# Moving the roots' write, three key transfers and four weight pieces to other places in the queues

## The chip, the cores and the metric

The kernel runs on one core of one Trainium2 chip. The metric is the device time of one execution in microseconds. The engines are TensorE (PE), VectorE (DVE), ScalarE (ACT), GpSimd (POOL) and SyncE (SP); transfers are issued by SP or by POOL, each of which has its own queue, and are carried out by 16 DMA engines.

## The reference

```python
def _attn_ref(q, k, v, g_norm):          # 8 images, 8 heads, 576 tokens, 64 wide
    kv = np.einsum('bhsd,bhse->bhde', k, v)
    out = np.einsum('bhsd,bhde->bhse', q, kv)
    rms = np.sqrt(np.mean(out * out, axis=-1, keepdims=True) + 1e-06)
    return out / rms * g_norm
# x = attention's result as (4608 tokens, 512)
# then two layers, each with its own w_in (512, 2048) and w_out (2048, 512):
#   layer 0: h = x @ w_in; x = (h * sigmoid(1.702 h)) @ w_out
#   layer 1: h = x @ w_in; x = (h - tanh(h)) @ w_out
```

Linear attention without softmax, a root-mean-square norm for each token and head, and two fully connected layers over all 4608 tokens.

## The kernel before

**The work.** The tokens are cut into eight images of 576 (n = 0 to 7). The program runs layer 0 over all images, then layer 1. Each image has a stage M1 (the product with `w_in` and the nonlinearity, in 54 steps and two tail steps that run inside M2) and a stage M2 (the product with `w_out`, 28 steps). From image 2 on, both stages use a scheme of seven products for a 2 x 2 block multiplication, so their operands are sums and differences that DVE makes. Every operand is split into a high and a low fp16 half; a product is three matmuls of 288 columns. A step of M1 has six matmuls, a step of M2 twelve.

**Weights.** M1's weights lie in `wi[0]` to `wi[7]`. In image 7 of layer 0 they are replaced by those of layer 1: `reload(p)` (L721) loads `wi[p]` through SP when M1 has finished with it. M2's weights don't stay: they stream through the ring `st` of four slots, in 14 pieces of 512 KB for each image, by `stream` (L879) on SP. The first four are issued after M1 in program order; each odd step of M2 up to 19 issues one more into the slot that it has freed. A slot holds weights for two steps. Since SP finds nothing else to wait for in images 2 to 6, it issues their first four pieces as soon as the slots are free, during the M2 before.

**Attention beside it.** While layer 0 works on image n, the attention of image b = n + 1 is prepared, as generators that are advanced a given number of times per step. `front(b)` runs in M1 at 0.56 a step: it multiplies keys by values (`head_products`, L446) and queries by the result, squares, and ends with `inverse_roots`, DVE instructions (L545) that make the inverse roots of the means in a tile `t`. The roots then go to DRAM (`rd`, L557, POOL) and are read back by four broadcasts of 288 KB that spread each row over 64 partitions (`broadcast`, L569, POOL); with 25 advances at 0.56 this falls on M1's step 45. `back(b)` runs in M2 at 1.12 a step: it waits eight advances, scales the attention's result by the roots (L712, two DVE instructions), makes M1's operands of the next image (`merged`) and then calls `fetch(b + 1)`, which loads for the image after that: unit 0 of keys and values (640 KB each), queries 0 (576 KB), unit 1, queries 1, unit 2, in this order, all on POOL; unit 3 is loaded by `front` when unit 0 has been used. The units go into the operand tile `xo` that the current image's M1 has finished with.

**Others in the queues.** A converter of layer 1's weights (`conv1`) runs in M1 at 0.7 an advance and none in M2: two loads of raw weights (L151, L152), DVE and ACT instructions of which the last is L184, and a write of the result to DRAM (L244 or L247), all its transfers on POOL. M2 stores its result `x2d` from `mscratch` on SP (L945), at steps 10, 22 and 26 and at the end; M1 copies its partial sums into `mscratch` (L806).

**Order.** Within one image PE, SP and POOL keep the order of the program; where instructions of the next image fall between them is the compiler's choice, as is the order on DVE and ACT, apart from this: an advanced generator's instruction on an engine isn't put ahead of the last main instruction emitted there.

```python
            for _ in range(min(FREED2.get(i, 0), 14 - len(pre))):
                pre.append(stream(l, len(pre)))
            due(i)
```

Of the kernel before, what the change touches and what calls it, by code (L numbers as in the profile page):

```python
# [20 lines left out]
T = 576  # L21
NS = NTOK // T
# [62 lines left out]
def body(ctx, tc, att, atp, gn, con, w_in, w_out, w2_in, w2_out, outT):  # L85
    nc = tc.nc
# [13 lines left out]
    rx, rs, rw, rq0, rq1, rk = (Scratch(scratch[:, a:z], z - a) for a, z in  # L100
                                ((0, 8 * H), (8 * H, 12 * H), (8 * H, 16 * H), (12 * H, 16 * H), (12 * H, 20 * H), (16 * H, SCRATCH)))
    xk = [Scratch(t.rearrange("p a b c d -> p (a b c d)").bitcast(F32), 14 * H) for t in xo]
    qs_of = lambda b: rq0 if b < 3 else rq1
    kvs_of = lambda b: rk if b < 2 else xk[b % 2]
# [8 lines left out]
    rd = dp.tile([NB, P, H], F32, name="rd")  # L113
# [198 lines left out]
    made, spare, pre, waiting = [0, 0], [], [], [1]  # L312
# [73 lines left out]
            ex = yield from scr.need(3 * H)  # L386
            yield from xprep(xb, ex, dst[:, kt])

    def part(b, kt, reg, a, n):
        t = yield from reg.need(n)  # L390
        nc.gpsimd.dma_start(out=t.ap[:, 0:n], in_=atp[b - 1, kt, :, a:a + n])
        return t

    def queries(b, kt):
        return part(b, kt, qs_of(b), 0, 2 * T)

    def unit_kv(b, u):
        return part(b, u // 2, kvs_of(b), 2 * T + u % 2 * 1280, 1280)

    def fetch(b):  # L400

        kvs, qs = [(yield from unit_kv(b, 0))], []
        yield
        qs.append((yield from queries(b, 0)))
        yield
        if b > 2:
            kvs.append((yield from unit_kv(b, 1)))
            yield
            qs.append((yield from queries(b, 1)))
            yield  # L410
            kvs.append((yield from unit_kv(b, 2)))
            yield
        ahead[b] = kvs, qs

# [127 lines left out]
    def inverse_roots(b):  # L542

        y, t = (yield from rq1.need(H)), (yield from rq1.need(H))
        stt = lambda o, a, s, b_, op0, op1: nc.vector.scalar_tensor_tensor(out=o, in0=a, scalar=s, in1=b_, op0=op0, op1=op1)  # L545
        nc.vector.tensor_scalar(out=y.ap.bitcast(U32), in0=ms.bitcast(U32), scalar1=1, scalar2=0x7fffffff,
                                op0=ALU.logical_shift_right, op1=ALU.bitwise_xor)
        for k, s in enumerate((SG, 0.375 * SG)):
            stt(t.ap, y.ap, s, ms, ALU.mult, ALU.mult)
            stt(t.ap, y.ap, s, t.ap, ALU.mult, ALU.mult)  # L550
            yield
            if k == 0:
                stt(t.ap, t.ap, -10.0 / 3.0, t.ap, ALU.add, ALU.mult)
                stt(y.ap, t.ap, 5.0, y.ap, ALU.add, ALU.mult)
        stt(t.ap, t.ap, -3.0, y.ap, ALU.add, ALU.mult)
        y.free()
        nc.gpsimd.dma_start(out=rd[b], in_=t.ap)  # L557
        t.free()
        yield
        yield from broadcast(b, rq1)  # L560

    def broadcast(b, other):

        rows = rd[b].rearrange("(g r) n -> r g n", r=32)
        rbs[b] = []
        for kt, reg in ((0, rs), (1, other)):
            t = yield from reg.need(4 * H)
            for c in range(2):
                nc.gpsimd.dma_start(out=t.ap[c * HD:(c + 1) * HD, :].rearrange("p (g n) -> p g n", g=4),  # L569
                                    in_=rows[2 * kt + c].partition_broadcast(HD))  # L570
            rbs[b].append(t)

    rbs = {}

    def unit0(u):

# [127 lines left out]

    def back(b, dst):

        for _ in range(8):
            yield
        x = xbs[b].ap.rearrange("p (k n) -> p k n", k=2)
        for kt in range(2):  # L710
            rb = rbs[b][kt]
            nc.vector.scalar_tensor_tensor(out=x[:, kt], in0=rb.ap, scalar=0.375 * SG, in1=x[:, kt], op0=ALU.mult, op1=ALU.mult)  # L712
            rb.free()
            yield
        yield from merged(b, dst, rq1)
        if b < NS - 1:
            yield from fetch(b + 1)
# [30 lines left out]
    def add_side(g, *rates):  # L748
        side.append([g, rates, 0.0])
        return g  # L750
# [125 lines left out]
    def stream(l, i):  # L876
        s = ST[sn[0] % 4]
        sn[0] += 1
        nc.sync.dma_start(out=s, in_=wod[l][WO[PIECES[i][0]], :, PIECES[i][1] * 4:PIECES[i][1] * 4 + 4])  # L879
        return s  # L880
# [258 lines left out]
    def both(b, *a):  # L1139
        yield from front_early(b)  # L1140
        fronted.append(b)
        yield from back_early(b, *a)
# [93 lines left out]
    for l in range(2):  # L1236
        for n in range(NS):
            bk = fr = None
            if l == 0:
                if n == 0:  # L1240
                    bk = add_side(both(1, xo[1]), 0.58, 1.12)
                elif n == 1:
                    bk = add_side(both(2, xo[0]), 1.05, 1.4)
                elif n < NS - 1:
                    fr = add_side(front(n + 1), 0.56, 0.0)
                else:
                    bk = add_side(x2load(0, xo[0]), 0.4, 0.8)
            elif n < NS - 1:
                bk = add_side(x2load(n + 1, xo[(n + 1) % 2]), 0.4, 0.8)
            if (l, n) == (0, 2):  # L1250
                rate(later, 0.7, 0.0)
            if (l, n) == (0, 7):
                rate(later, 0.6, 0.55)
                while converted[0] < 16:
                    next(later)

            def hook(p):
                if (l, n) == (0, NS - 1) and p >= 2:
                    reload(p - 2)
                if p >= 2 and p % 2 == 0:  # L1260
                    jcap[0] = (1, 2, 5)[p // 2 - 1]
                    jadvance(jcap[0])

            if (l, n) == (1, 0):
                rate(later, 0.35, 0.0)
            jpos[:] = [0, 0, 0]
            jcap[0] = 0
            if (l, n) == (0, 0):
                def ahead_of(p):
                    adv(2 * p + 2)  # L1270

                def behind(p):
                    if p == 1:
                        withdraw(extra)
                    elif 4 <= p < 7:
                        operand(p - 4)

                def at_step(k):
                    if k % 4 == 0 and k < 32:
                        adv(min(32, 18 + k // 2))  # L1280
                    if k == 23:
                        adv(32)
                        start_sums()
                    pace(1.9 if k < 23 else 0)

                m1_plain(0, ahead_of, lambda p: pace(2.5), behind)
                m2_halves(at_step)
                drain([bk])
                continue
            man = ExitStack()  # L1290
            if (l, n) == (0, 1):
                nop = lambda p: None

                def behind(p):
                    raw_out(p)
                    if 4 <= p < 7:
                        operand8(p - 4)

                m1_plain(1, nop, nop, behind)
                raw_out(NP)  # L1300
                while 2 not in fronted:
                    next(bk)
                while made[1] < NP:
                    next(dfr[0])
                own.extend([jx[:, 0:1024], jx[:, 1152:2176]] + k4(stf, 2))
                todo_in.extend(range(NP))
                next(dfr[0])
                rate(dfr[0], 0.7, 1.8)
                waiting.clear()
                add_side(later, 0.0, 0.9)  # L1310
                m2_plain8(1)
                drain([bk])
                start.close()
                continue
            else:
                if (l, n) > (1, 0):
                    fixed[0] = True
                    marks.clear()
                    marks.update({k: m for k, m in latest.items() if k == ENG.DVE})
                man.enter_context(tc.manual_schedule(engines=frozenset([ENG.PE, ENG.SP, ENG.Pool])))  # L1320
                tails = m1(l, n, hook)
            jcap[0] = 5
            if (l, n) == (1, 0):
                drain([later])
            if (l, n) == (0, 2):
                upto(NP)
            if not pre:
                pre.extend(stream(l, i) for i in range(4))
            if l == 0 and 1 < n < NS - 1:
                drain([fr])  # L1330
                bk = add_side(back(n + 1, xo[(n + 1) % 2]), 0.0, 1.12)
            if l == 0 and n == NS - 1:
                reload(NP - 2)
                fr = add_side(last_reload(), 0.0, 1.0)
            m2(l, n, tails, pre)
            pre.clear()
            drain([bk, fr])
            man.close()
# [46 lines left out]
```

## Time and profile before

| | |
|---|---|
| time, median of 3 runs | 1457.34 us (1457.29 to 1457.53) |
| the profiled execution's own time | 1458.78 us |
| its span, first to last instruction | 1457.0 us |
| mean granted TensorE clock | 0.996 |
| PE, DVE, ACT busy | 98%, 77%, 60% |
| SP's queue, POOL's queue | 165.82 MB, 86.38 MB |

The span is what the profile's times refer to, from the first instruction; the execution's own time has 1.8 us around it. A busy share is over the whole span. A wait of an engine is listed with what ended it.

### The profile page before, as it was taken

The numbers are of one execution on the slowest core, as the hardware profiler recorded it, in microseconds if no ns is written. First come the engines' busy times: TensorE is split into PE (matmuls) and PEld (weight loads), VectorE is DVE, ScalarE is ACT, GpSimd is POOL, SyncE is SP. The second block draws the span as 40 slices with busy tenths as digits, with TensorE's granted clock in tenths as the row PEclk, the third lists the DMA queues.
The fourth block names the chain that finished last, engine by engine and source line by source line (L and its number), as shares of the span: only waits on it lengthen the run. The fifth ranks groups of instructions, "written<-read, shape, count | busy, mean of one in ns | idle before, by whom it ended". The sixth has DMA issues, their size and how long they took to land.

```text
span 1457.0 us, 30035 instructions
## 1 busy us (share of the span) xinstructions
PE 1428.0 (98%) x11970; PEld 1108.4 (76%) x11970; DVE 1118.0 (77%) x2122; ACT 873.1 (60%) x1906; POOL 170.0 (12%) x266
## 2 busy tenths in 40 slices
PE   7999999999999999999989999999999999999998
PEld 5777777777777777767767777777777777777777
DVE  4996468896977959769786977878687777878485
ACT  5784645765757657476664746556564656555463
POOL 1322011211201123121120000000000000000000
PEclk9999999999999999999999999999999999999999
DMA  9895784466572764846696252432506052332404
GB/s 320 297 337 176 232 289 166 140 234 224 174 282 97 234 221 113 301 145 189 206 322 201 86 196 82 137 124 87 190 31 209 29 181 72 126 111 75 161 27 151
DMA packets 96732, 254.10 MB, mean 174 GB/s; under 512 B 10864, under 2 KB 44784, under 8 KB 96592
## 3 DMA queue, kind: packets, MB, share of 16 engines
q1 hardware_dynamic: 73824, 165.82, 34.6%
q0 software_dynamic: 22768, 86.38, 17.8%
q8 instruction: 93, 1.52, 0.4%
q14 instruction: 47, 0.39, 0.1%
HBM read 200.79 MB, written 51.36 MB: 173 GB/s over the span
## 4 chain that ended last, share of the span: by engine, by line
PE 87%; DMA 7%; DVE 3%; ACT 3%; issue 1%; SPq 0%; ACTq 0%; DVEq 0%
PE X L773 7%; PE X L774 7%; PE X L775 7%; PE X L963 7%; PE X L965 7%; PE X L964 7%; DMA st<-wod 5%; PE Z L773 4%; PE Z L775 4%; PE Z L774 4%; PE Y L963 3%; PE Y L965 3%; PE Y L964 3%; PE Y L773 2%; PE Y L775 2%; PE Y L774 2%
## 5 line engine op out<-in xcount | busy, mean ns | idle before, releaser
L852 ACT ACTIVATE jt<-gt 128x576 f16<-128x576 f32 x392 | 266.3, 682 | 173.8 <-PE X L965 55.3
L858 DVE SCALAR_TENSOR_TENSOR jt<-gt,jt 128x576 f16<-128x576 f32 x392 | 290.5, 751 | 65.4 <-ACT jt L852 63.5
L773 PE MATMUL X<-xo,wi 128*128 128x288 f16 x896 | 256.8, 287 | 1.2 <-ACT mscratch L806 1.0
L963 PE MATMUL X<-jt,st 128*128 128x288 f16 x896 | 256.6, 286 | 1.4 <-DMA st<-wod 1.4
L774 PE MATMUL X<-xo,wi 128*128 128x288 f16 x896 | 256.6, 286 | 0.0
L965 PE MATMUL X<-jt,st 128*128 128x288 f16 x896 | 256.5, 286 | 0.0
L964 PE MATMUL X<-jt,st 128*128 128x288 f16 x896 | 256.5, 286 | 0.0
L775 PE MATMUL X<-xo,wi 128*128 128x288 f16 x896 | 256.5, 286 | 0.0
L773 PEld LDWEIGHTS <-wi 128*128 128x128 f16 x1568 | 152.9, 98 | 52.8 <-issue 13.4
L963 PEld LDWEIGHTS <-st 128*128 128x128 f16 x1568 | 153.1, 98 | 51.6 <-DMA st<-wod 12.5
L806 ACT COPY mscratch<-X 128x288 f32<-128x288 f32 x336 | 132.9, 397 | 91.9 <-PE X L775 89.2
L774 PEld LDWEIGHTS <-wi 128*128 128x128 f16 x1568 | 153.0, 98 | 41.2 <-issue 2.9
L965 PEld LDWEIGHTS <-st 128*128 128x128 f16 x1568 | 153.2, 98 | 39.4
L964 PEld LDWEIGHTS <-st 128*128 128x128 f16 x1568 | 153.1, 98 | 39.1
L775 PEld LDWEIGHTS <-wi 128*128 128x128 f16 x1568 | 153.0, 98 | 39.2
L838 DVE TENSOR_TENSOR gt<-gt 128x576 f32<-128x576 f32 x224 | 164.0, 749 | 1.9 <-ACT gt L780 1.6
L811 DVE TENSOR_TENSOR mscratch<-Z,mscratch 128x288 f32<-128x288 f32 x224 | 101.4, 453 | 61.0 <-PE Z L775 30.1
L963 PE MATMUL Y<-jt,st 128*128 128x288 f16 x448 | 128.9, 288 | 3.7 <-DMA st<-wod 3.7
L964 PE MATMUL Y<-jt,st 128*128 128x288 f16 x448 | 128.9, 288 | 0.0
L965 PE MATMUL Y<-jt,st 128*128 128x288 f16 x448 | 128.9, 288 | 0.0
L773 PE MATMUL Z<-xo,wi 128*128 128x288 f16 x448 | 128.4, 287 | 0.2 <-DVE mscratch L811 0.2
L774 PE MATMUL Z<-xo,wi 128*128 128x288 f16 x448 | 128.3, 286 | 0.0
(315 smaller groups left out, 2634.0 us busy)
## 6 DMA issues: line engine op xcount, KB each, us to landing
st<-wod SPq DMA_DIRECT2D x196, 512.0 KB, 4.4
xo<-atp POOLq DMA_DIRECT2D x24, 640.0 KB, 8.9
scratch<-x2d SPq DMA_DIRECT2D x32, 288.0 KB, 5.0
scratch<-atp POOLq DMA_DIRECT2D x14, 576.0 KB, 7.3
scratch<-rd POOLq DMA_DIRECT2D x28, 288.0 KB, 7.9
outT<-mscratch POOLq DMA_DIRECT2D x28, 288.0 KB, 4.5
wi<-wid SPq DMA_DIRECT2D x8, 896.0 KB, 6.2
x2d<-mscratch SPq DMA_DIRECT2D x24, 288.0 KB, 4.8
```

The costliest lines, as they stand in the source:

```text
L773: nc.tensor.matmul(out=out, lhsT=wh, rhs=xh, start=fresh and kt == 0, stop=False, skip_group_check=k)
L774: nc.tensor.matmul(out=out, lhsT=wh, rhs=xl, start=False, stop=False, skip_group_check=k)
L775: nc.tensor.matmul(out=out, lhsT=wl, rhs=xh, start=False, stop=kt == 1, skip_group_check=k)
L806: main(nc.scalar.copy(out=b.ap, in_=x))
L811: main(nc.vector.tensor_tensor(out=b.ap, in0=add[0], in1=b.ap, op=ALU.add))
L838: tt = lambda o, a, b: main(nc.vector.tensor_tensor(out=G[:, :, o, :], in0=G[:, :, a, :], in1=G[:, :, b, :], op=ALU.subtract))
L852: main(nc.scalar.activation(out=j[:, :, 0, :], in_=GT[STEPS2[i][1]][:, :, QD[STEPS2[i][0]], :], func=AF.Copy, scale=SX))
L858: main(nc.vector.scalar_tensor_tensor(out=j[:, :, 1, :], in0=GT[STEPS2[i][1]][:, :, QD[STEPS2[i][0]], :], scalar=SX, in1=j[:, :, 0, :], op ...
L963: nc.tensor.matmul(out=out, lhsT=wh, rhs=xh, start=a, stop=False, skip_group_check=k)
L964: nc.tensor.matmul(out=out, lhsT=wh, rhs=xl, start=False, stop=False, skip_group_check=k)
L965: nc.tensor.matmul(out=out, lhsT=wl, rhs=xh, start=False, stop=z, skip_group_check=k)
```

## The change

Three things move.

- The roots' write and the four broadcasts leave `inverse_roots`, which now only keeps the tile in `root[b]`; `back` issues them at its first advance, after M2's step 0.
- In `fetch` for images 4 to 7, units 0, 1 and 2 of keys and values are issued by SP (`nc.sync`) instead of POOL. Their place in the program is the same, the advances from M2's step 22 on. Queries and unit 3 stay on POOL.
- In image 7 of layer 0, the first four pieces of the stream are issued after M1's last step for p = 2, ahead of `reload(0)`, instead of after M1.

```diff
--- before.py
+++ after.py
@@ -386,29 +386,30 @@
             ex = yield from scr.need(3 * H)
             yield from xprep(xb, ex, dst[:, kt])
 
-    def part(b, kt, reg, a, n):
+    def part(b, kt, reg, a, n, e=None):
         t = yield from reg.need(n)
-        nc.gpsimd.dma_start(out=t.ap[:, 0:n], in_=atp[b - 1, kt, :, a:a + n])
+        (e or nc.gpsimd).dma_start(out=t.ap[:, 0:n], in_=atp[b - 1, kt, :, a:a + n])
         return t
 
     def queries(b, kt):
         return part(b, kt, qs_of(b), 0, 2 * T)
 
-    def unit_kv(b, u):
-        return part(b, u // 2, kvs_of(b), 2 * T + u % 2 * 1280, 1280)
+    def unit_kv(b, u, e=None):
+        return part(b, u // 2, kvs_of(b), 2 * T + u % 2 * 1280, 1280, e)
 
     def fetch(b):
 
-        kvs, qs = [(yield from unit_kv(b, 0))], []
+        e = nc.sync if b > 3 else nc.gpsimd
+        kvs, qs = [(yield from unit_kv(b, 0, e))], []
         yield
         qs.append((yield from queries(b, 0)))
         yield
         if b > 2:
-            kvs.append((yield from unit_kv(b, 1)))
+            kvs.append((yield from unit_kv(b, 1, e)))
             yield
             qs.append((yield from queries(b, 1)))
             yield
-            kvs.append((yield from unit_kv(b, 2)))
+            kvs.append((yield from unit_kv(b, 2, e)))
             yield
         ahead[b] = kvs, qs
 
@@ -554,10 +555,7 @@
                 stt(y.ap, t.ap, 5.0, y.ap, ALU.add, ALU.mult)
         stt(t.ap, t.ap, -3.0, y.ap, ALU.add, ALU.mult)
         y.free()
-        nc.gpsimd.dma_start(out=rd[b], in_=t.ap)
-        t.free()
-        yield
-        yield from broadcast(b, rq1)
+        root[b] = t
 
     def broadcast(b, other):
 
@@ -570,7 +568,7 @@
                                     in_=rows[2 * kt + c].partition_broadcast(HD))
             rbs[b].append(t)
 
-    rbs = {}
+    rbs, root = {}, {}
 
     def unit0(u):
 
@@ -704,6 +702,9 @@
 
     def back(b, dst):
 
+        nc.gpsimd.dma_start(out=rd[b], in_=root[b].ap)
+        root[b].free()
+        yield from broadcast(b, rq1)
         for _ in range(8):
             yield
         x = xbs[b].ap.rearrange("p (k n) -> p k n", k=2)
@@ -1255,6 +1256,8 @@
                     next(later)
 
             def hook(p):
+                if p == 2 and (l, n) == (0, NS - 1):
+                    pre.extend(stream(l, i) for i in range(4))
                 if (l, n) == (0, NS - 1) and p >= 2:
                     reload(p - 2)
                 if p >= 2 and p % 2 == 0:
```

## Rows read from the trace of the kernel before

**Rows 1.** The page: busy time of each engine (share of the span), instructions.
```profile
PE 1428.0 (98%) x11970; PEld 1108.4 (76%) x11970; DVE 1118.0 (77%) x2122; ACT 873.1 (60%) x1906; POOL 170.0 (12%) x266
```

**Rows 2.** Waits, whole span, PE and PEld: total us, times, longest us.
```profile
PE Z L963 <- DMA st<-wod: 4.8, 3, 2.3
PE Y L963 <- DMA st<-wod: 3.7, 1, 3.7
...
PE X L963 <- DMA st<-wod: 1.4, 2, 0.9
...
PEld L963 <- DMA st<-wod: 12.5, 9, 4.0
```

**Rows 3.** Chain that ended last: start us, length us, what.
```profile
302.99 9.69 DMA st<-wod
...
391.98 9.62 DMA st<-wod
...
480.30 11.76 DMA st<-wod
...
577.07 10.44 DMA st<-wod
...
739.78 9.86 DMA st<-wod
```

**Rows 4.** SP's timeline, image 7: start us, us, engine, line, what.
```profile
706.54 0.94 SPq L383 DMA_DIRECT2D scratch<-x2d  x2
713.10 5.47 SPq L721 DMA_DIRECT2D wi<-wid  x2
...
723.97 15.76 SPq L721 DMA_DIRECT2D wi<-wid  x4
739.78 2.87 SPq L879 DMA_DIRECT2D st<-wod  x4
```

**Rows 5.** POOL's timeline, begin of image 2's M2 and its end.
```profile
294.99 0.56 POOL L557 DMA_DIRECT2D rd<-scratch  x1 [7.70 <-DVE cbk L181]
297.56 0.63 POOL L569 DMA_DIRECT2D scratch<-rd  x1 [2.01 <-PE Z L775]
...
301.85 0.57 POOL L244 DMA_DIRECT2D wid<-third  x1
...
303.83 0.55 POOL L391 DMA_DIRECT2D xo<-atp  x1
330.40 0.55 POOL L391 DMA_DIRECT2D scratch<-atp  x1 [26.02 <-ACT mscratch L906]
```

**Rows 6.** DMA queues from 671 to 674 us: packets, MB, share of 16 engines.
```profile
q0 software_dynamic: 206, 0.76, 103.4%
q1 hardware_dynamic: 2, 0.00, 0.4%
```

**Rows 7.** One window of the busy times, its last columns the clock, DMA share, GB/s.
```profile
335.00:341.00 6.00, 6.00 (x77) 4.62 (x76) 1.35 (x5) 2.16 (x6) 0.53 (x1) 1.00 1.03 407
```

**Rows 8.** SP's timeline at the end of image 2's M2.
```profile
328.82 0.37 SPq L945 DMA_DIRECT2D x2d<-mscratch  x1
```

**Rows 9.** Chain that ended last, first product with keys in image 3's M1.
```profile
337.92 0.73 PE AT L446 x20
```

**Rows 10.** Line 391, queries and units: time from issue to landing.
```profile
DMA to landing us min/median/max: 4.0/8.0/15.2
```

**Rows 11.** DVE's timeline, begins of M2 in images 2 and 3.
```profile
295.98 1.09 DVE L184 TENSOR_TENSOR third<-cbk,third 128x896 f16<-128x896 f32 x1 [0.27 <-ACT third L239]
...
309.87 1.36 DVE L712 SCALAR_TENSOR_TENSOR scratch<-scratch 128x1152 f32<-128x1152 f32 x1 [1.13 <-DMA scratch<-rd]
...
387.56 1.08 DVE L184 TENSOR_TENSOR cbk<-cbk 128x896 f16<-128x896 f32 x1
```

**Rows 12.** POOL's timeline, end of image 3's M1: the roots' write.
```profile
384.12 0.56 POOL L557 DMA_DIRECT2D rd<-scratch  x1 [1.73 <-DVE scratch L545]
```

**Rows 13.** Line 806, copies to mscratch: what ended ScalarE's idle time, us, times.
```profile
  DMA x2d<-mscratch: 1.3, 2
```

## The prediction

> **What bounds the kernel now.** I read the busy times first. TensorE (PE) is busy for 1428.0 of 1457.0 us [rows 1], so a change that doesn't touch its 11970 matmuls can win at most what PE stands still. The same row gives the tempo: 1428.0 / 11970 = 0.119 us a matmul, so an M2 step of 12 matmuls lasts 1.43 us. Next I read PE's waits, to see which of the idle time has a cause that the diff touches. The largest causes are stream pieces, the second layer's weights that M2 reads through the ring `st`: 4.8 us in three waits (Z, the longest 2.3), 3.7 in one (Y), 1.4 in two (X, the longer 0.9) [rows 2]. Then the chain that ended last, to place them: long pieces stand on it at 303, 392, 480, 577 and 740 us [rows 3], each early in M2 of images 2, 3, 4, 5 and 7. They took 9.6 to 11.8 us. A ring slot freed after step 1, 3 or 5 is needed six steps later, 6 x 1.43 = 8.6 us, so each is late by some 1 to 3 us, as PE's waits say. X's second wait (1.4 - 0.9 = 0.5) is no part of these five. So 4.8 + 3.7 + 0.9 = 9.4 us are at stake. The weight loads' wait for pieces, 12.5 us [rows 2], says that the true figure may be a little more.
>
> Last I read what the pieces compete with. In image 7 SP's timeline answers: the first four pieces are issued at 739.78, behind six reloads, the last of which waits for M1 to be done with `wi[5]` [rows 4]. In the others it is traffic: POOL issues the roots' broadcasts at 297.56, then a conversion write, two loads and a unit of keys at 303.83 [rows 5]. While broadcasts run (671 to 674, image 6), POOL's queue takes all of the DMA engines and SP's 0.4% [rows 6].
>
> **The change, part by part.**
>
> *Image 7's first pieces.* They move ahead of reload 0. SP is free from 706.54 + 0.94 = 707.5 and reload 0 goes out at 713.10, when its wait ends [rows 4]. Four issues took 2.87 us in the same rows, so they fit in that gap and delay no reload. Their 4 x 524 KB need 5.2 us at 407 GB/s, the rate of a stretch with both queues full [rows 7]. They have until 739.78 + 9.86 - 3.7 = 745.9, over 30 us. The whole 3.7 us goes. If the slots were still in use the issue would slip, but the previous M2 has ended by then. What is late next is the fifth piece, which has its usual six steps. Gain 3.7.
>
> *Units 0 to 2 of the keys go through SP (images 2 to 5).* Unit 0 leaves the begin of M2, where POOL issued it at 303.83 without a wait. On SP it is emitted at step 22, behind the last piece and the store of step 22. Its 655 KB are 655 / 407 = 1.6 us of all DMA engines, which the late pieces get back. Against the stalls: image 2 has 0.9, all freed; the longest of Z's three is 2.3, of which 1.6 go; its other two make 2.5 together, of which I take 2.4. Sum 0.9 + 1.6 + 2.4 = 4.9. Late next are the 0.8 or so left in Z's longest, and after that DVE, whose five operands of lead are counted below. Bounds: nothing, if the broadcasts alone decide; 5.7, if all goes (0.9 + 4.8). I take 4.9 because the unit lies in the same queue as the traffic that the pieces wait for.
>
> Does the unit come in time? In image 2 the store before it goes out at 328.82 and takes 0.37 [rows 8]; M1's first product with keys is at 337.92 [rows 9]. That leaves 8.7 us. All that runs then, three units and the two queries that POOL releases at 330.40 [rows 5], is 3.14 MB, 7.7 us at 407 GB/s, and unit 0 is first. I cost it at nothing. The other bound is the longest landing of such a transfer, 15.2 us [rows 10], 6.5 too late each time. I don't reach for it: units 1 and 2 and the queries already move in that stretch, only unit 0 is new.
>
> *The roots.* Their write and four broadcasts are taken from the end of `front` (M1, step 45) to the first step of `back`, which runs after M2's step 0. Within an image POOL keeps program order, so they are now behind the conversion's DMAs emitted in M1 and in its two tail steps. In image 2 the conversion write waits for its vector instruction (295.98 + 1.09 = 297.07 [rows 11]); with 0.57 for itself and 1.4 for the two loads (303.83 - 301.85 - 0.57 [rows 5]) the roots' write goes at 299.1 instead of 294.99, 4.1 later. In image 3 the same sum, 387.56 + 1.08 + 0.57 [rows 11], gives 389.2 instead of 384.12 [rows 12], 5.1 later. For images 4 to 6 I take the time as it is, since the write waits for the same roots. Who waits: the two scalings at L712, in VectorE's (DVE's) order with M2's operands behind them. The second already waits 1.13 us in image 2 [rows 11]. PE is covered by the operands made ahead, five steps or 7.2 us less the two scalings' own 2 x 1.36 [rows 11], so 4.5 us. 4.1 fits and 5.1 nearly does, since in image 3 the scalings have slack of their own that I don't count. Cost taken 0; the other bound is 4.1 + 5.1 = 9.2 us of PE.
>
> In exchange the conversions and loads no longer stand behind the broadcasts; the broadcasts' own bytes stay in M2's begin. I take neither gain nor loss from the shift: a piece that comes after the broadcasts meets an emptier queue, one that falls among them is held as before, as the two queues' shares in image 6 show (103.4% and 0.4%, [rows 6]).
>
> A rule weighs otherwise. The Trainium skill, "DMA: Bandwidth & Descriptors", section "Queues, rings and completion order", says that each DMA engine takes turns between the queues with work, packet by packet. By that the stream would keep about half beside the broadcasts, and the sum would be rival D's 9.4 us and not 8.6. The rows of image 6 show nothing like half, so I go by them.
>
> *Sum.* 3.7 + 4.9 = 8.6 us. The profiled execution took 1458.78 us (span 1457.0 and 1.8 around it), so it would be 1450.2. It lies 1.4 above the median of the runs, so against 1457.34 the forecast is **1448.7 us**.
>
> **The rivals.** The measurement can tell about 0.2% from no change, that is 2.9 us, or 1454.4 and below for faster.
>
> *A. The broadcasts still hold the stream off.* For it: 103.4% against 0.4% in image 6, where no unit was fetched [rows 6], and broadcasts that start 4 to 5 us later fall on the next piece. Against it: image 6 has those shares and still none of PE's waits. Then only image 7 wins: 1457.3 - 3.7 = 1453.6.
>
> *B. Late roots stall DVE.* Broadcasts 4.1 and 5.1 us later stop it at L712 and M2 runs out of operands. The full price, 9.2, would eat the gain: 1457.9. For it: the wait of 1.13 us that is there already. Against it: the 4.5 us of lead.
>
> *C. Slower: M2's last stores come after the units.* SP's ring now has 3 x 1.6 = 4.8 us of units ahead of the stores of step 26 and the end. M1's first copies to `mscratch` (L806) need the space that these stores empty, and 1.3 us of waits for them are there now [rows 13]. If the 4.8 us pass through to PE in images 3 to 6, the time is 1448.7 + 4 x 4.8 = 1467.9; from 8.6 / 4 = 2.2 us an image it decides the sign. Against it: today units 1 and 2 share the DMA engines with the same stores, so most of that delay is already paid. The same page and section of the Trainium skill says that a ring's descriptors are consumed in order, which speaks for C; no row here shows a store behind a unit in one ring.
>
> *D. All five stalls go.* If the stream moved on beside the broadcasts, only the bytes in the two queues would count; with the unit gone from M2's begin the pieces would be in time everywhere: 1457.3 - 9.4 = 1447.9. For it: image 6 has the broadcasts, no unit, and no piece among PE's waits (Z's three, Y's and X's are taken by the others). Against it: the shares in [rows 6]. This is what the rule of turns above would give.
>
> That the change doesn't do what it says would be the roots' write at its old time, because DVE finishes the roots that late; this changes nothing in the sum.
>
> **How the numbers follow.** Forecast 0.51, A 0.18, B 0.07, C 0.07, D 0.10, and 0.07 for ScalarE and DVE instructions that fall in another order, either way. The range goes from 1446.0 (a gain of 11.3, D with most of what the weight loads' 12.5 us [rows 2] has over PE's 9.4) to 1454.8 (A and a microsecond of B or C); 0.8 of the chance lies in it. Faster: forecast, D, most of A and part of the last, 0.80. Same: the rest of A, B, some of C, 0.11. Slower: 0.09.
>
> **What would show it.** Right: no wait for `st<-wod` at M2 of image 7, with its four pieces issued at about 708; the waits of images 2 to 5 at 1 us in all; units issued by SP near step 22; the roots' write 4 to 5 us later in images 2 and 3. Wrong: `PE <- DMA st<-wod` a step or two later than now (A), PE waiting for `jt` from L858 (B), PE or L806 waiting for x2d stores, or PE at L446 for the units (C).

## The result and the profile after

The changed kernel is slower: 1471.64 us median (1470.53 to 1477.36) against 1457.43 of the kernel before in the same set of runs, a ratio of 1.0099 with a 95% interval of 1.0079 to 1.0119. Forecast were 1448.7 us and a gain. The profiled execution took 1477.36 us, with a span of 1475.6; it was the slowest of the four, 5.7 us above the median, so its lines show more loss than the median has.

Line numbers from 387 on have shifted by one or two (L773 is L774, L806 is L807, L712 is L713; the broadcasts at L569 are L567, and the roots' write is L705). First the page's busy times, to be set beside [rows 1].

```profile
PE 1434.5 (97%) x11970; PEld 1114.4 (76%) x11970; DVE 1117.9 (76%) x2122; ACT 872.0 (59%) x1906; POOL 163.4 (11%) x254
```

The same 11970 matmuls keep PE busy 6.5 us longer, and its idle time has grown from 1457.0 - 1428.0 = 29.0 to 1475.6 - 1434.5 = 41.1 us, 12.1 more. Together these are the 18.6 us by which the span has grown. The idle part is in PE's list of waits (total us, times, longest), which answers to [rows 2].

```profile
PE X L774 <- ACT mscratch L807: 14.5, 8, 4.0
PE X L964 <- DMA st<-wod: 3.4, 3, 1.6
...
PE X L965 <- DVE jt L859: 1.8, 2, 1.3
...
PE AT L447 <- DMA xo<-atp: 1.1, 2, 0.7
PE Z L964 <- DMA st<-wod: 1.0, 2, 0.5
```

Of the waits for stream pieces, Y's 3.7 of image 7 is gone, as forecast; those of images 2 to 5 (X and Z) have 4.4 instead of 5.7, where the forecast left about 1. And 14.5 us of another kind stand at the top: PE waits in M1 for ScalarE to copy a partial sum out of bank X (L807), for which it waited 1.0 us before. What ScalarE itself waited for there, over the whole span, answers to [rows 13], where it was 1.3 us.

```profile
  PE X L776: 86.4, 159
  DMA x2d<-mscratch: 19.4, 4
```

So the copies wait for M2's stores of `x2d` to leave `mscratch`, 19.4 us in four waits, one at the begin of each M1 that follows an M2 with units on SP. SP's timeline at the end of image 2's M2 shows the queue, and ScalarE's shows the first of the four waits.

```profile
334.16 0.37 SPq L946 DMA_DIRECT2D x2d<-mscratch  x1
334.58 1.47 SPq L391 DMA_DIRECT2D xo<-atp  x3
336.15 0.38 SPq L880 DMA_DIRECT2D st<-wod  x1
337.63 0.38 SPq L946 DMA_DIRECT2D x2d<-mscratch  x1
```

```profile
344.21 0.38 ACT L807 COPY mscratch<-X 128x288 f32<-128x288 f32 x1
...
350.44 0.40 ACT L807 COPY mscratch<-X 128x288 f32<-128x288 f32 x1 [5.44 <-DMA x2d<-mscratch]
```

Three units lie ahead of the store of step 26. It is issued at 337.63, ScalarE is free for M1's third copy at 350.44 - 5.44 = 345.0, and the place is free only at 350.4, when the store has landed 12.7 us after its issue. That is rival C, at the place that the prediction gave it.

In the kernel before, the same store is issued at 332.30 and the same copy runs at 341.84, when PE has finished its bank, without a wait for the store:

```profile
332.30 0.37 SPq L945 DMA_DIRECT2D x2d<-mscratch  x1
```

```profile
341.84 0.40 ACT L806 COPY mscratch<-X 128x288 f32<-128x288 f32 x1 [0.62 <-PE X L775]
```

```profile
DMA to landing us min/median/max: 9.0/10.5/12.0
```

The last line is of the two stores issued from 330 to 350 us; the first of them, that of step 26, took the 9.0 us. So it landed at 341.3, half a microsecond before its place was wanted. In images 2 to 5 the store of step 26 took 9.0 to 10.8 us to land in the kernel before and 12.1 to 15.7 in the changed one.

The 6.5 us of longer matmuls are the clock. PE's wait at that place, then one window of the busy times after it, columns as in [rows 7], and the same view of the kernel before, behind the 3.7 us wait of image 7:

```profile
350.89 0.40 PE L774 MATMUL X<-xo,wi 128*128 128x288 f16 x1 [3.84 <-ACT mscratch L807]
```

```profile
349.50:356.30 6.80, 5.41 (x26) 2.75 (x26) 1.55 (x2) 3.35 (x9) 1.86 (x3) 0.50 0.48 190
```

```profile
749.60:753.00 3.40, 3.31 (x14) 2.09 (x15) 0.00 (x0) 0.15 (x1) 0.00 (x0) 0.50 1.05 424
```

PEclk is 0.50: TensorE was granted 1.2 instead of 2.4 GHz. In the first window 26 matmuls start in 6.8 us, of which PE is busy for 5.41; 1 / 0.119 a us would have made 57 in the whole of it. Two more stretches at half clock that the kernel before doesn't have, one in M2 of image 2 and one behind the copies' wait in image 6's M1:

```profile
318.00:322.50 4.50, 4.43 (x24) 2.85 (x23) 4.50 (x6) 1.09 (x2) 0.00 (x0) 0.62 0.87 305
```

```profile
643.00:646.50 3.50, 3.50 (x20) 1.66 (x18) 1.01 (x5) 1.08 (x4) 0.00 (x0) 0.51 0.13 49
```

A last one, of the same length, lies at 452 to 455 us, behind the wait in image 4's M1, and image 7's is gone. So 6.8 us and three stretches of some 3.4 have come and one of 3.4 has left; at half clock that is (6.8 + 3 x 3.4 - 3.4) / 2 = 6.8 us, near the 6.5.

The roots come later than worked out. POOL's timeline of image 2, to be read beside [rows 5], and the two scalings with their waits, beside [rows 11]:

```profile
297.53 0.56 POOL L244 DMA_DIRECT2D wid<-third  x1 [10.09 <-DVE third L184]
298.08 0.56 POOL L705 DMA_DIRECT2D rd<-scratch  x1
304.59 2.48 POOL L567 DMA_DIRECT2D scratch<-rd  x4 [5.95 <-PE X L966]
```

```profile
313.68 1.36 DVE L713 SCALAR_TENSOR_TENSOR scratch<-scratch 128x1152 f32<-128x1152 f32 x1 [6.05 <-DMA scratch<-rd]
...
317.93 1.36 DVE L713 SCALAR_TENSOR_TENSOR scratch<-scratch 128x1152 f32<-128x1152 f32 x1 [0.16 <-DMA scratch<-rd]
```

The write is 3.1 us later than before, the broadcasts 7.0 (304.59 - 297.56). The broadcasts wait for the write to land, which took 3.9 us here and 2.0 before; the other 2 us the profile lists as a wait for PE, and what was waited for there isn't shown. DVE stands 6.05 us at the first scaling.

### The profile page after: what moved, and what is told of

It is laid out like the page before. It is cut to its first block, busy times and chain, and to the rows that moved or that the text cites. A ratio compares the mean times of both kernels' runs of the same rounds, so it can differ in the third digit from the quotient of the medians.

```text
span 1475.6 us, 30050 instructions
## 1 busy us (share of the span) xinstructions
PE 1434.5 (97%) x11970; PEld 1114.4 (76%) x11970; DVE 1117.9 (76%) x2122; ACT 872.0 (59%) x1906; POOL 163.4 (11%) x254
## 4 chain that ended last, share of the span: by engine, by line
PE 71%; DMA 10%; DVE 9%; issue 5%; ACT 3%; POOL 1%; SPq 1%; DVEq 0%; ACTq 0%; POOLq 0%
PE X L774 7%; PE X L776 6%; PE X L775 6%; PE X L966 5%; PE X L964 5%; PE X L965 5%; DMA x2d<-mscratch 4%; PE Z L774 3%; PE Z L775 3%; PE Z L776 3%; PE Y L966 3%; PE Y L965 3%; PE Y L964 3%; DVE jt L859 2%; DMA scratch<-rd 2%
## 5 line engine op out<-in xcount | busy, mean ns | idle before, releaser
L774 PE MATMUL X<-xo,wi 128*128 128x288 f16 x896 | 257.5, 287 | 14.7 <-ACT mscratch L807 14.5
L807 ACT COPY mscratch<-X 128x288 f32<-128x288 f32 x336 | 132.9, 398 | 106.9 <-PE X L776 86.4
L774 PEld LDWEIGHTS <-wi 128*128 128x128 f16 x1568 | 154.0, 98 | 53.9 <-issue 14.3
L774 PE MATMUL Z<-xo,wi 128*128 128x288 f16 x448 | 129.1, 288 | 0.2 <-DVE mscratch L812 0.2
L775 PE MATMUL Z<-xo,wi 128*128 128x288 f16 x448 | 128.9, 288 | 0.0
L776 PE MATMUL Z<-xo,wi 128*128 128x288 f16 x448 | 128.8, 287 | 0.0
L964 PE MATMUL Y<-jt,st 128*128 128x288 f16 x448 | 128.1, 286 | 0.0
L965 PE MATMUL Y<-jt,st 128*128 128x288 f16 x448 | 128.1, 286 | 0.0
```

Source lines behind the costliest of these rows:

```text
L774: nc.tensor.matmul(out=out, lhsT=wh, rhs=xh, start=fresh and kt == 0, stop=False, skip_group_check=k)
L775: nc.tensor.matmul(out=out, lhsT=wh, rhs=xl, start=False, stop=False, skip_group_check=k)
L776: nc.tensor.matmul(out=out, lhsT=wl, rhs=xh, start=False, stop=kt == 1, skip_group_check=k)
L807: main(nc.scalar.copy(out=b.ap, in_=x))
L964: nc.tensor.matmul(out=out, lhsT=wh, rhs=xh, start=a, stop=False, skip_group_check=k)
L965: nc.tensor.matmul(out=out, lhsT=wh, rhs=xl, start=False, stop=False, skip_group_check=k)
```

## Experiments

Two theories. **Ring**: the stores stand behind the units in SP's ring, M1's copies wait for the stores, PE for the copies, and its clock falls. **Roots**: the late write and broadcasts make everything behind them late. A third, **bytes**, came with the first results: the DMA engines are full at the end of M2 whichever ring the units lie in. Each ratio is to the kernel before in the same set of runs (medians 1458.3 to 1459.5 us), with a 95% interval.

**The parts alone.** The units:

```diff
+        (e or nc.gpsimd).dma_start(out=t.ap[:, 0:n], in_=atp[b - 1, kt, :, a:a + n])
...
+        e = nc.sync if b > 3 else nc.gpsimd
```

> The kernel before with the units of keys through SP alone; roots and image 7's pieces as before. Ring theory (M2's last stores wait behind three units in SP's ring, and M1's copies to mscratch wait for the stores): the waits of M1's copies for x2d stores are there as after the whole change, some 15 to 20 us on ScalarE, and the time is 1468 to 1474 us. Roots theory (the late write and broadcast make everything behind them late): no such waits, and the unit taken from M2's begin gives up to 5 us, 1452 to 1457.

Measured: 1.0041 (1.0025 to 1.0058), 1463.77 us. The copies' waits for stores, and PE's for the copies:

```profile
  DMA x2d<-mscratch: 11.9, 4
```

```profile
PE X L774 <- ACT mscratch L807: 5.7, 7, 2.5
```

With no root moved the waits are there, so the roots theory falls as the whole cause. But they are smaller than expected, and so is the loss. The pieces' waits, which the unit's leaving should have cut by 4.9 us, are 3.5 (Z, of which 0.4 in image 6) and 1.2 (X), so 4.3 in images 2 to 5 against 5.7.

The roots:

```diff
-        nc.gpsimd.dma_start(out=rd[b], in_=t.ap)
-        t.free()
-        yield
-        yield from broadcast(b, rq1)
+        root[b] = t
...
     def back(b, dst):
+        nc.gpsimd.dma_start(out=rd[b], in_=root[b].ap)
+        root[b].free()
+        yield from broadcast(b, rq1)
```

> The kernel before with the roots' write and broadcasts at M2's begin alone. Ring theory: only M2 of images 2 and 3 suffers, by some 2 us each, and the others gain a little: 1456 to 1462 us, no wait of M1's copies for stores beyond the 1.3 us of before. Roots theory: 1468 us or more.

Measured: 1.0030 (1.0017 to 1.0042), 1462.50 us, a little above the expected range. The line of the scalings (L712) has four waits for the broadcasts, where the kernel before had one of 1.1 us:

```profile
  DMA scratch<-rd: 13.0, 4
```

Of the 5.0 us by which the profiled span grew, 3.1 are longer matmuls, with new stretches at half clock in M2 of images 2 and 3, and 1.7 are PE waiting for DVE's operands (`jt`). The pieces' waits of images 2 to 5 are 5.5 in all, nearly as before, but have moved: 1.8 and 2.0 in images 2 and 3, 1.3 and 0.4 in 4 and 5. The copies wait 3.5 us for stores, more than the 1.3 that were expected.

The pieces:

```diff
+                if p == 2 and (l, n) == (0, NS - 1):
+                    pre.extend(stream(l, i) for i in range(4))
```

> The kernel before with image 7's first four pieces early alone. Both theories: the wait of 3.7 us at M2 of image 7 goes and with it the 3.4 us at half clock behind it, worth 1.7 us more: 1451.5 to 1453.5 us. If something else was as late as the pieces there, 1455 or more.

Measured: 0.9983 (0.9969 to 0.9996), 1455.32 us; that is a gain of 2.5 us, between 0.6 and 4.5. Image 7's wait is gone from the profile and so is the half clock behind it, but the gain is less than the 4 to 6 us expected and falls where something else was to be as late; the profile names no such wait, and its execution, 1451.97 us, was the quickest of ten. What this kernel still has of the pieces' waits serves as a measure for the others, since no unit and no root moved in it:

```profile
PE Z L963 <- DMA st<-wod: 3.0, 2, 2.0
...
PE X L963 <- DMA st<-wod: 1.4, 1, 1.4
```

That is 4.4 us in images 2 to 5. So the 4.3 with the units gone shows nothing of the 4.9.

**The whole without one part.** Units back on POOL:

```diff
-        e = nc.sync if b > 3 else nc.gpsimd
+        e = nc.gpsimd
```

> The changed kernel with the units back on POOL; roots and pieces as changed. Ring theory: the waits of M1's copies for stores fall back to about 1 us and the time to 1451 to 1457 us, so that the units explain all of the loss. Roots theory: 1465 us or more. If the loss needs both (late roots and units), it lies between.

Measured: 1.0006 (0.9995 to 1.0018), 1459.54 us; the copies' waits for stores are 5.6 us. Both lie above what the ring theory expected, the time between the two theories. At the top of PE's waits stands DVE, the sign of rival B:

```profile
PE X L964 <- DVE jt L858: 5.8, 4, 3.6
```

Late roots and early pieces cancel; the units bring the loss from 0.06 to 1.0%. They cost more than the 0.41% that they cost alone. Hence the opposite, roots back where they were:

> The changed kernel with the roots where they were: units through SP and image 7's pieces early. The parts alone are worth +0.41, +0.30 (roots) and -0.17 per cent, 0.54 together, and the whole costs 1.0. If late roots and units aggravate each other (the roots push M2's last stores closer to the copies that wait for them), this kernel is as the sum of its two parts, 1.001 to 1.004 of before, with 10 to 13 us of the copies' waits for stores. If units and early pieces aggravate each other instead, 1.006 to 1.008.

Measured: 1.0023 (0.9999 to 1.0046), 1462.22 us, the sum of its two parts (0.41 - 0.17 = 0.24%). The copies' waits, 8.9 us, are below the expected 10 to 13; this profiled execution, 1454.38 us, was the quickest of ten. So it is roots and units that aggravate each other (both without the early pieces weren't run). The rows of image 2 say how. With the units alone, the store of step 26 is issued at 332.18 and ScalarE is free for the third copy at 345.47 - 4.12 = 341.35, 9.2 us later; in the whole change it is 345.0 - 337.63 = 7.4 us. In both the store needs about 13 us. DVE, which stood at the scalings, makes the last results 5.5 us later (336.79 against 331.34), M1's copies come only 3.7 us later, and the store has less time. In image 3 its time shrinks too, from 10.3 to 7.3 us. In images 4 and 5 it doesn't; there the store takes longer to land (14.1 and 15.7 us against 13.2 and 11.8), for a reason that no row shows.

```profile
332.18 0.46 SPq L946 DMA_DIRECT2D x2d<-mscratch  x1
```

```profile
345.47 0.40 ACT L807 COPY mscratch<-X 128x288 f32<-128x288 f32 x1 [4.12 <-DMA x2d<-mscratch]
```

```profile
DMA to landing us min/median/max: 11.9/12.6/13.2
```

(All of the kernel with the units alone; the last is of its two stores from 330 to 350 us, of which that of step 26 took 13.2.)

**The link between units and copies.** Four kernels of one set; the first is the change itself.

> The changed kernel itself, as the measure for the other three of this set: 1.0 per cent above the kernel before, about 1471 us, with M1's copies waiting 15 to 20 us for x2d stores in four waits.

Measured: 1.0101 (1.0068 to 1.0135), 1474.05 us, with 20.3 us of the copies' waits for stores.

The units in a ring of their own:

```diff
-        e = nc.sync if b > 3 else nc.gpsimd
+        e = nc.scalar if b > 3 else nc.gpsimd
```

> The changed kernel, with the units issued by ScalarE, so that they lie in a ring of their own and neither SP's stores nor POOL's queries stand behind them; the same bytes at about the same time. Ring theory: the copies' waits for stores fall from about 19 us to under 8, and the time to 1459 to 1463 us (the late roots stay). Bytes theory (the DMA engines are full at the end of M2, whichever ring the units are in): the waits stay over 15 us and the time at 1468 or more.

Measured: 1.0027 (1.0011 to 1.0042), 1463.92 us. The copies' waits are halved and PE's for the copies fall from 15.2 to 4.7:

```profile
  DMA x2d<-mscratch: 9.9, 5
```

```profile
PE X L774 <- ACT mscratch L807: 4.7, 6, 2.3
```

The ring of their own is worth 10 us of the 14.6, though both the waits and the time are a little above what was expected. The stores of step 26 land after 10.3 to 11.7 us, near the 9.0 to 10.8 of the kernel before. Of the 9.9 us of waits left, most go with the late roots, since 5.6 are there with the units on POOL; the rest may be the bytes' share. One thing differs beside the ring: in image 2 ScalarE issues unit 0 at 330.16, 4.4 us sooner than SP does in the changed kernel (334.58), so the bytes are not quite at the same time.

One more place in `mscratch`:

```diff
-SCRATCH, MAIN = 5896, 7 * 288
+SCRATCH, MAIN = 5896, 8 * 288
```

> The changed kernel with mscratch of 8 instead of 7 places, so that M1's first copies find a place whose store has long landed. If the stores are what PE waits for at M1's begin, by way of the copies, the copies' waits fall to under 6 us and the time to 1459 to 1464 us, though the stores land as late as in the changed kernel. If the stores' wait is only listed there and something else is as late, the time stays at 1468 or more.

Measured: 1.0020 (1.0005 to 1.0035), 1462.68 us; 7.9 us of the copies' waits, more than the expected 6, and 3.1 of PE's. The units lie in SP's ring as in the change, and the stores of step 26 land as late (12.6 to 15.0 us); the copies no longer need that place so soon, and most of the loss is gone.

Units behind the stores:

```diff
...
+            while not stored[0]:
+                yield
+            for u in range(3):
+                kvs.append((yield from unit_kv(b, u, e)))
...
```

`stored[0]` is set when the last store of M2 has been issued; the two queries, on POOL, are now emitted ahead of the units.

> The changed kernel with the units still on SP but emitted after M2's last store. Ring theory: the copies' waits for stores fall to under 6 us, and PE waits for unit 0 at the first product with keys instead, 2 to 5 us in each of four images: 1464 to 1474 us. Bytes theory: the stores stay late as well, and both waits are seen: 1475 or more.

Measured: 1.0233 (1.0204 to 1.0261), 1491.94 us, above the range. No copy waits for a store any more, and PE stands at the first product with keys, where it waits for unit 0:

```profile
PE AT L458 <- DMA xo<-atp: 28.1, 4, 7.7
```

7 us each, and beyond the waits PE's matmuls are 9.2 us longer than in the kernel before (1437.2 against 1428.0 us busy), which is the clock. A window behind the second of these waits, PEclk 0.71 over 10 us:

```profile
451.00:461.00 10.00, 9.80 (x89) 6.86 (x90) 1.81 (x6) 3.68 (x10) 0.53 (x1) 0.71 0.46 165
```

So with all three units on SP either the stores or the units are late.

**A smaller dose.** Unit 0 alone on SP, with the early pieces:

```diff
+        kvs, qs = [(yield from unit_kv(b, 0, e))], []
...
             kvs.append((yield from unit_kv(b, 1)))
```

> The kernel before with image 7's pieces early and unit 0 alone through SP; units 1 and 2 stay on POOL, the roots stay where they were. Only 1.6 us of units then lie in SP's ring ahead of the stores instead of 4.8. Ring theory: the copies' waits for stores fall from the 11.9 us of the units alone to 2 to 6 us, and the time is 0.998 to 1.001 of before. Bytes theory (unit 0's bytes are the only new ones in M2's end, and all of them are there): the waits stay near 12 us and the time at 1.002 or more.

Measured: 0.9969 (0.9953 to 0.9985), 1454.99 us; the copies' waits are 3.1 us, as the ring theory has it (the time is even a little better), though unit 0's are the only bytes that are new in M2's end. And again the pieces got nothing from its leaving:

```profile
PE X L964 <- DMA st<-wod: 0.8, 1, 0.8
...
PE Z L964 <- DMA st<-wod: 4.0, 2, 2.1
```

4.8 us beside the 4.4 of the early pieces alone.

**The opposite of the roots' move.** Roots sooner, with the early pieces:

```diff
-                fr = add_side(front(n + 1), 0.56, 0.0)
+                fr = add_side(front(n + 1), 0.68, 0.0)
```

> The opposite of the roots' move: front advances at 0.68 instead of 0.56 a step, so that the roots' write and the broadcasts are emitted at M1's step 37 instead of 45; image 7's pieces early, units on POOL. If the broadcasts are what the pieces wait for at M2's begin, most of the 6 us of waits for pieces in images 2 to 5 go: 0.993 to 0.996 of before. If the unit of keys behind them is the cause, or if VectorE can't finish the roots sooner, as with the pieces alone: 0.997 to 0.999.

Measured: 0.9907 (0.9872 to 0.9942), 1446.66 us, faster than both kernels and a little better than expected. POOL's timeline of image 2 has the write 8.7 us and the first broadcast as much sooner than [rows 5], and of PE's waits for pieces one is left in the list, of 0.4 us:

```profile
286.27 0.56 POOL L557 DMA_DIRECT2D rd<-scratch  x1 [8.41 <-DVE scratch L545]
288.86 1.86 POOL L569 DMA_DIRECT2D scratch<-rd  x3 [2.03 <-DMA rd<-scratch]
```

```profile
PE X L963 <- DMA st<-wod: 0.4, 1, 0.4
```

The units of keys are on POOL at M2's begin here, as before (image 2's at 300.39 instead of 303.83). So it was the broadcasts that the pieces waited for, and not the unit; the faster front brings the conversion's write and loads forward too, which no run parts from the broadcasts. The profiled span is 11.9 us shorter than that of the kernel before: PE stands still for 9.1 us less, which is the pieces' waits, and its matmuls take 2.8 us less, which goes with the clock (0.998 against 0.996).

With the eighth place of `mscratch` added:

> The same with mscratch of 8 places. The waits of M1's copies for stores are only 1 to 3 us in the kernel before, so little is left to win by it: as the one without, or up to 0.001 less. If the room changes the order of ScalarE's and VectorE's work for the worse, up to 0.002 more.

Measured: 0.9915 (0.9885 to 0.9944), 1446.72 us: no difference.

## Why the prediction was wrong

**The units' time on SP, costed at nothing: the step that failed.** The unit itself did come nearly in time (1.1 us of PE at L447). What wasn't charged is what stands behind the units: the stores of step 26 and the end, and behind them M1's copies. The prediction had this as rival C, with its place and its full price, and set it at 0.07 with one argument: that units 1 and 2 share the DMA engines with the same stores already, so that most of the delay is paid. That argument asked for the wrong thing. Most of the store's time was indeed there already: with the units in POOL's queue the store of step 26 took 9.0 us in image 2. But the copy wanted its place 9.5 us after the issue (332.30 to 341.84), which left half a microsecond for any more, and behind the units the store takes 12.7 (13.2 with the units alone). Units alone on SP: 11.9 us of waits. In a ring of their own, or with a place more in `mscratch`: most of the loss gone. The Trainium skill's rule that a ring's descriptors are consumed in order ("DMA: Bandwidth & Descriptors", section "Queues, rings and completion order") agrees with the runs: behind the units the stores landed after 12.1 to 15.7 us, with the units in another ring after 10.3 to 11.7. C's break-even, 2.2 us an image, was passed: 14.5 - 1.0 = 13.5 us of PE in four images, 3.4 each.

**The 4.9 us for the unit's leaving M2's begin: wrong.** With the unit gone the pieces' waits of images 2 to 5 are 4.3 us (units alone) and 4.8 (unit 0 alone), and 4.4 where no unit moved: none of the 4.9 came. Rival A was right here, the broadcasts decide as far as the runs part them, and the run with sooner roots shows it from the other side. The figure took the unit's 1.6 us of DMA time off the stalls without asking whether the unit's bytes moved before the piece that was late. In the kernel before they moved mostly after it. Image 2's late piece landed at 302.99 + 9.69 = 312.7 [rows 3]; the unit, issued at 303.83 behind the broadcasts and two loads in POOL's queue, took 13.5 us and landed at 317.3:

```profile
xo<-atp POOLq DMA_DIRECT2D x1, 640.0 KB, 13.5
```

**The roots, cost taken 0: mis-sized.** The delay of the write in image 2 was forecast as 4.1 and is 3.1, since the two loads that the sum put ahead of it came behind it. Left out was that the broadcasts wait for the write to land, which took 3.9 us instead of 2.0; with the 2 us that stay unexplained they are 7.0 us late, more than the 4.5 that the operands cover. Alone the move costs 0.30%, 4.2 us, half of rival B's full price. B's own sign, PE waiting for `jt`, is 1.7 us of it and 5.8 with the early pieces added; the rest of the cost alone is mostly half clock behind such waits and the pieces'. In the whole the late roots also make the stores late, and so C worse.

**Image 7: right.** The pieces were issued before reload 0, the wait of 3.7 us is gone, and alone the part gives 2.5 us (0.6 to 4.5), which allows the 3.7 but doesn't show all of it.

**Not in the sum at all: the clock.** Behind some of PE's waits lies a stretch at half clock: in the change behind those of 3.8, 2.8 and 4.1 us for copies and not behind that of 1.5; in the kernel before behind image 7's 3.7 and not behind image 4's 2.3. The change's 18.6 us of span are 12.1 of waiting and 6.5 of this. By the same reckoning image 7's wait was worth up to 3.7 + 1.7 us, but the gain of the pieces alone, at most 4.5, doesn't bear that out.

**The sum of the parts** (0.41 + 0.30 - 0.17 = 0.54%) is half of the whole (1.0%). The runs without one part put the rest on roots and units together; that the stores' shorter time is the way is read from the rows of images 2 and 3 and wasn't tried by itself, and why the stores land later in images 4 and 5 is open. Open, too, is how much of the waits left with the units in ScalarE's ring (9.9 us) is the bytes' share.

## What to carry to other kernels

Before a transfer is moved into another queue, list what that queue issues after it and who waits for that, down to the buffer that a store must empty. Then ask how much slack is left, not how much of the delay is there already: a store of 9.0 us was hidden with half a microsecond to spare, and one of 13 wasn't. Find which of several transfers really holds a late one, by moving one at a time, before crediting the move of another. Where bulk traffic collides with a stream, try first to bring it sooner, into a stage that streams nothing: 0.68 in place of 0.56, with image 7's pieces early, gave 13.6 us (8.5 to 18.7), where the whole change was forecast to give 8.6.

## What the runs showed of the hardware

Beside POOL's broadcasts SP's stream came nearly to a stop ([rows 6]), though two of its pieces were under way: issued at 670.2 and 673.1, they took 8.8 and 7.4 us to land, and the next ones 5.7 and 5.1. Moved 8.7 us ahead of the stream in image 2, the same broadcasts left 0.4 us of waits for pieces in the whole profile. Beside other loads of POOL's queue, the conversion's and the unit of keys, the stream kept its half. From 310 to 313 us, in image 2 of the kernel before, columns as in [rows 6]:

```profile
q0 software_dynamic: 164, 0.61, 52.1%
q1 hardware_dynamic: 161, 0.59, 50.9%
```

So it was not any traffic of the other queue that held the stream off. TensorE was granted 1.2 GHz for 6.8 us after a wait of 3.8 us, and for 3.4 us after one of 3.7, so that the first wait cost up to 6.8 / 2 = 3.4 us more than its own length and the second up to 3.4 / 2 = 1.7.
